# Tail copies on VectorE, one eviction per step, joined q and v loads, and weights written in place, in an attention and gated feed-forward kernel

## The chip, the cores and the metric

The kernel runs on one core of one Trainium2 chip. The metric is the device time of one execution in microseconds (us). The kernel before took 737.65 us, the median of 3 runs (736.29 to 739.47).

## The reference, cut to what matters

```python
# q, k, v: (4 batches, 8 heads, 576 positions, 64), float32
scores = q @ k.T / 8 + bias        # bias per head: a two-layer net of log positions (hidden 32)
attn = exp(scores - max) / (sum + 1e-9)
x = (attn @ v) -> (2304 tokens, 512)
h = x @ w_in                       # (2304, 2048), weights arrive in float64
g = (a0 + a1*h + a2*h^2 + a3*h^3) / (1 + |b0|*|h| + |b1|*h^2 + 1e-6)
out = g @ w_out                    # (2304, 512)
```

## The kernel before, in words

The work has three stages. From 0 to about 54 us a table of the position bias is computed and stored in device memory. From about 54 to 323 us attention runs. After that the feed-forward part runs to the end, at 735.5 us; it multiplies each weight as a high and a low part, since the products run in a reduced 32-bit format.

Attention goes by 16 units of one head pair and one batch (`units`), and a unit has five steps (`steps`, c = 0 to 4). In steps c = 0 to 3 TensorE multiplies 128 query rows of each of the two heads with all 576 keys; in step c = 4 it takes the last 64 rows of both heads at once. The order is written out by hand in `step_a(i)`, and each engine works strictly in that order:

- `e_qk(i)` (L328): the score products, into one PSUM tile `sc` per head, of two banks each. There are only two such buffers, so a step's products for a head must wait until the previous step's tile for that head is no longer read.
- `e_ttr(i, j)` (L356): VectorE adds the bias to `sc`, writes the sum `s2` and its extreme value. `e_exp` (L371): ScalarE takes the exponential.
- `e_tp(i - 2)` (L415): TensorE transposes the exponentials of two steps ago, 64 rows at a time (r = 0, 1). Two of these transposes (the "tails", the last 64 keys) go into free columns of the present step's `sc` tiles (`spare`, L346), the others into `tp`, one bank for each r. ScalarE copies tail r = 0 to `ptl` and both `tp` tiles to `ptm` (L552); VectorE copies tail r = 1 (L564), after both `e_ttr` and, in step c = 0, after the two small operations of `e_recip`. Accesses of two engines to one PSUM bank are put in series: `e_ttr` of head 0 therefore waits for ScalarE's copy of tail r = 0 out of the same tile.
- `e_pv` (L462): products with v, some in each step (`PV_KEYS`). `e_pvout` copies the result, and one unit later `e_norm` multiplies it by the reciprocal sums, which make a trip through device memory (`rs`, `rb`).

SyncE issues nearly all transfers from one queue in written order. Each takes one of eight semaphores in turn and its issue waits until the transfer eight places earlier has landed. Per unit there are the loads of q, k and the 64-row ends `qdg` (`load_qk`, four transfers) and of v and its ends `vdg` (`load_v`, three). Beside attention run the weight jobs (`w_conv`): 128 columns of `w_in` or rows of `w_out` (`f`, `part`) are loaded, split by VectorE and ScalarE into high `wh` and low `wl`, and stored to a scratch tensor `ws` in device memory (`w_out_to`, L105). `w_load` (L217) brings them back into the resident tiles `wih`, `wil`, `woh`, `wol` of a weight group (two `f` each). The loads stand in the SyncE queue at places given by `after` (L641). VectorE's parts of the jobs are spread over the steps by `JOB_OPS`.

Of the kernel before, what the change touches and what calls it, by code (L numbers as in the profile page):

```python
# [8 lines left out]
F32 = mybir.dt.float32  # L9
F32R = mybir.dt.float32r  # L10
# [6 lines left out]
P = 128  # L17
# [17 lines left out]
def tile_attn_moe(  # L35
# [75 lines left out]
    def w_conv(f, part):  # L111
        st = {}

# [48 lines left out]
        def low():  # L162
            V.scalar_tensor_tensor(
                out=tl("wl", F32R), in0=st["wm"], scalar=2.0 ** -36, in1=st["wk"].bitcast(F32),
                op0=ALU.mult, op1=ALU.mult,
            )

        def store():
            w_out_to(
                f, part, st["wh"].rearrange("p (k f) -> p k f", k=KD),  # L170
                st["wl"].rearrange("p (k f) -> p k f", k=KD),
            )
# [48 lines left out]
    with tc.manual_schedule():  # L221
# [3 lines left out]
        with ExitStack() as actx:  # L225
# [3 lines left out]
            ps_tp = actx.enter_context(tc.tile_pool(name="ps_tp", bufs=2, space=PSUM))  # L229
            ps_pv = actx.enter_context(tc.tile_pool(name="ps_pv", bufs=1, space=PSUM))  # L230

            vdg = [cpool.tile([P, P], F32, tag=f"vdg{i}", name=f"vdg{i}") for i in range(3)]
            qdg = [apool.tile([P, P], F32, tag=f"qdg{i}", name=f"qdg{i}") for i in range(2)]
            sums = [apool.tile([P, P], F32, tag=f"sum{i}", name=f"sum{i}") for i in range(2)]
            for t in vdg + qdg + sums:
                G.memset(t, 0.0)
# [21 lines left out]
            def load_qk(u, eng=nc.sync):  # L258
                p, b = units[u]
                q = qkp.tile([P, 512], F32, tag="q", name=f"q{u}")  # L260
                k = qkp.tile([P, KW], F32, tag="k", name=f"k{u}")
                eng.dma_start(out=q, in_=qt[b, p, :, 0:512])
                eng.dma_start(out=k, in_=kt[b, p])
                for j in range(2):
                    r = slice(64 * j, 64 * j + 64)
                    eng.dma_start(out=qdg[u % 2][r, r], in_=qt[b, p, r, 512:S])
                qk[u] = (q, qdg[u % 2], k)

            def load_v(u):
                p, b = units[u]  # L270
                t = qkp.tile([P, 4, P], F32, tag="v", name=f"v{u}", bufs=3)
                nc.sync.dma_start(out=t, in_=vp[b, p, 0:512].rearrange("(c k) d -> k c d", k=P))
                dg = vdg[u % 3]
                for j in range(2):
                    nc.sync.dma_start(
                        out=dg[64 - 64 * j:P - 64 * j, 64 * j:64 * j + 64],
                        in_=vp[b, p, 512:576, 64 * j:64 * j + 64],
                    )
                vt[u] = (t, dg)
# [76 lines left out]
            def e_ttr(i, j):  # L356
                u, c = steps[i]
                p, b = units[u]
                t = epool.tile([P, S], F32, tag="s2", name=f"s2_{i}_{j}")
                m = epool.tile([P, 1], F32, tag="m", name=f"m{i}_{j}", bufs=4)  # L360
                idx = 8 if j == 2 else 4 * j + c
                V.tensor_tensor_reduce(  # L362
                    out=t.rearrange("p (a s) -> p a s", a=2),
                    in0=sc.pop((i, j))[:, :, :SH],
                    in1=bias[p][:, idx, :].rearrange("p (a s) -> p a s", a=2),
                    scale=-0.125, scalar=3.0e38,
                    op0=ALU.add, op1=ALU.min, accum_out=m,
                )
                s2[i, j] = (t, m)
# [45 lines left out]
            def e_tp(i, tl):  # L415
# [7 lines left out]
                ps = [ps_tp.tile([P, 8, 64], F32, tag="tp", name=f"tp{i}_{r}") for r in range(2)]  # L423
# [5 lines left out]
                if c < 4:  # L429
                    for r in range(2):  # L430
                        tr(r, tl[r], 512)
                    for kc in range(4):
                        for j in range(2):
                            for r in range(2):
                                tr(r, ps[r][:, 2 * kc + j, :], (S + 64 if j == 0 else 0) + kc * P)
                    return (
                        [(pl[:, o:o + 64], tl[0])]
                        + [(pm[:, :, :, o + 64 * r:o + 64 * r + 64],
                            ps[r].rearrange("p (k j) s -> p k j s", j=2)) for r in range(2)],
                        [(V.tensor_copy, pl[:, o + 64:o + P], tl[1])], None,  # L440
                    )
# [8 lines left out]
                for r in range(2):  # L450
                    x = slice(64 * r, 64 * r + 64)
                    T.transpose(ps[r][:, 5, :], sm[x, :], ident[x, x])  # L452
                return (
                    [(pm[:, :, r, o:o + 64], ps[r][:, 0:4, :]) for r in range(2)],
                    [(eng, rt[:, 64 * r:64 * r + 64], ps[r][0:9, 5, :])
                     for r, eng in ((0, A.copy), (1, V.tensor_copy))]
                    + [(eng, pl[x, o:o + 64], ps[r][x, 4, :])
                       for r, x, eng in ((0, slice(64, P), A.copy), (1, slice(0, 64), V.tensor_copy))],
# [61 lines left out]
            def step_a(i):  # L520
# [70 lines left out]
            with ExitStack() as bctx:  # L591
# [21 lines left out]
                pc = ps_tp.tile([P, 512], F32, tag="tp", name="pc")  # L613
# [41 lines left out]
                for y, n in enumerate(order):  # L655
# [4 lines left out]
                    if 24 <= n < 32:  # L660
                        ps = ps_tp.tile([P, 512], F32, tag="tp", name=f"pb{n}")
# [40 lines left out]
            w_alloc(wpool, 2)  # L702

# [196 lines left out]
def _layout(inputs):  # L900
# [8 lines left out]
    qt = np.concatenate([q0, q1], axis=2)  # L909
# [7 lines left out]
    vp = np.asarray(inputs["v"]).reshape(B, NP, 2, S, D).transpose(0, 1, 3, 2, 4).reshape(B, NP, S, 2 * D)  # L917
# [49 lines left out]
```

## Time and profile before

| | before |
|---|---|
| median of 3 runs | 737.65 us |
| the profiled execution | 737.32 us, span 735.5 us |
| TensorE matmul busy | 706.6 us (96%) |
| VectorE busy | 594.6 us (81%) |
| ScalarE busy | 515.6 us (70%) |
| GpSimd busy | 187.2 us (25%) |
| share of the chain that ended last | PE 75%, DMA 8%, DVE 5%, ACT 3%, SyncE's queue 2% |

In the profile PE is TensorE, PEld its weight loads, DVE VectorE, ACT ScalarE, POOL GpSimd, SPq the queue of SyncE. Busy time of PE counts a matmul from start to modelled end, so a PE that is "busy" may still be held up inside a row. "[0.41 <-ACT ptl L552]" behind a row says that the engine sat idle for 0.41 us before it and what ended the idle time.

### The profile page before, as it was taken

What the parts mean: (1) busy time and instruction counts of PE and PEld (TensorE: products, weight loads), DVE (VectorE), ACT (ScalarE), POOL (GpSimd) and SP (SyncE); (2) the same over time, 40 slices, a digit from 0 to 9 for tenths busy, and PEclk for the clock granted to TensorE, in tenths of its full rate; (3) what the DMA queues carried; (4) which work ended last, traced back from release to release, by engine and by line L of the source; (5) the groups of instructions that cost most, each with busy time, mean ns of one, the idle gap of its engine ahead of it and who ended that gap; (6) DMA issues with size and microseconds to landing.
All of it is one profiled execution on the core that took longest, in us unless ns stands there. A gap on an engine that the chain in (4) does not pass through costs nothing.

```text
span 735.5 us, 13700 instructions
## 1 busy us (share of the span) xinstructions
PE 706.6 (96%) x4930; PEld 545.4 (74%) x4930; DVE 594.6 (81%) x1068; ACT 515.6 (70%) x969; POOL 187.2 (25%) x127
## 2 busy tenths in 40 slices
PE   6988999998999999899999999999999999999997
PEld 3225666665666566568788999889999899988996
DVE  7995677776677777649999999999997878788766
ACT  6889888887788787757566665767665665556552
POOL 0000000000000000004544444554543444344442
PEclk9999999999899999999999999999999999999999
DMA  4787879988798888847434444457942213031021
GB/s 162 274 317 262 265 250 285 298 270 258 249 310 274 251 291 266 267 118 241 129 129 150 146 145 172 160 173 238 284 166 86 89 40 130 2 128 59 29 86 43
DMA packets 107427, 137.76 MB, mean 187 GB/s; under 512 B 17104, under 2 KB 66528, under 8 KB 107360
## 3 DMA queue, kind: packets, MB, share of 16 engines
q1 hardware_dynamic: 106768, 136.11, 56.6%
q8 instruction: 39, 0.64, 0.4%
q10 hardware_dynamic: 592, 0.78, 0.3%
q14 instruction: 28, 0.23, 0.1%
HBM read 94.96 MB, written 41.90 MB: 186 GB/s over the span
## 4 chain that ended last, share of the span: by engine, by line
PE 75%; DMA 8%; DVE 5%; ACT 3%; issue 2%; SPq 2%; POOL 0%; DVEq 0%; ACTq 0%; POOLq 0%
PE o L803 25%; PE h L316 24%; PE sc L341 10%; PE pv L471 6%; PE tp L427 4%; PE pb L668 3%; DMA k<-in_kt_dram 2%; DVE s L362 1%; PE pv L477 1%; ACT p L382 1%; DMA ws<-wl 1%; DMA wy<-in_w_in_dram 1%; PE sc L427 1%; ACT ptm L552 1%; DMA rs<-rt 1%
## 5 line engine op out<-in xcount | busy, mean ns | idle before, releaser
L362 DVE CUSTOM_DVE_ANT_0 s<-sc,bias 128x576 f32<-128x576 f32 x144 | 104.1, 755 | 71.1 <-ACT ptl L552 61.2
L733 POOL TENSOR_TENSOR u<-u,w 128x768 f32<-128x768 f32 x48 | 96.6, 2013 | 159.3 <-ACT u L731 133.6
L341 PE MATMUL sc<-k,q 64*128 64x288 f32 x512 | 108.4, 439 | 9.9 <-DMA k<-in_kt_dram 4.4
L382 ACT ACTIVATE p<-s,m 128x576 f32<-128x576 f32 x144 | 111.7, 781 | 2.2 <-DVE m L362 1.8
L730 ACT ACTIVATE w<-h 128x768 f32<-128x768 f32 x48 | 39.0, 813 | 100.5 <-PE h L316 98.1
L772 POOL TENSOR_TENSOR gl<-m,r 128x768 fp32r<-128x768 f32 x47 | 87.1, 1853 | 71.5 <-DVE m L765 71.5
L316 PE MATMUL h<-xh,wg 128*128 128x384 f32 x384 | 101.7, 336 | 0.0
L341 PEld LDWEIGHTS sc<-k,q 64*128 64x128 f32 x512 | 60.0, 189 | 55.9 <-issue 23.8
L552 ACT COPY ptm<-tp 128x512 f32<-128x512 f32 (+1 forms) x160 | 79.1, 546 | 23.9 <-PE tp L452 12.6
L471 PE MATMUL pv<-ptm,v 128*64 128x320 f32 (+1 forms) x512 | 80.4, 425 | 0.0
L378 POOL MEMSET p<- 128x64 f32 x16 | 2.4, 151 | 305.7 <-ACT ptl L552 160.4
L803 PE MATMUL o<-wg,gh 128*128 128x512 f32 x288 | 79.0, 391 | 0.0
L737 ACT ACTIVATE r<-u,qc 128x768 f32<-128x768 f32 x48 | 45.1, 940 | 37.9 <-POOL u L733 37.3
L427 PE MATMUL tp<-ident,p 64*128 64x64 f32 x1184 | 70.3, 227 | 1.3 <-DVE ptl L564 0.7
L316 PEld LDWEIGHTS h<-xh,wg 128*128 128x128 f32 x384 | 69.7, 188 | 1.5 <-DMA rb<-rs 0.5
L758 DVE SCALAR_TENSOR_TENSOR m<-u,qc,gh 128x768 f32<-128x768 f32 x48 | 64.6, 1346 | 5.0
L741 DVE TENSOR_TENSOR t<-t,h 128x768 f32<-128x768 f32 x48 | 45.5, 948 | 27.0 <-ACT t L732 16.2
L316 PE MATMUL h<-xh,wih 128*128 128x384 f32 x192 | 64.9, 338 | 0.8 <-DVE t L744 0.8
L427 PEld LDWEIGHTS tp<-ident,p 64*128 64x128 f32 x1184 | 59.7, 140 | 7.9 <-ACT ptm L552 1.2
L316 PE MATMUL h<-xl,wih 128*128 128x384 f32 x192 | 64.7, 337 | 0.3 <-DVE xl L302 0.3
L316 PE MATMUL h<-xh,wil 128*128 128x384 f32 x192 | 64.7, 337 | 0.0
L316 PE MATMUL h<-xl,wg 128*128 128x384 f32 x192 | 64.4, 335 | 0.0
(82 smaller groups left out, 1412.6 us busy)
## 6 DMA issues: line engine op xcount, KB each, us to landing
tab<-e SPq DMA_DIRECT2D x36, 295.5 KB, 3.6
wx<-in_w_in_dram SPq DMA_DIRECT2D x16, 512.0 KB, 5.1
wy<-in_w_in_dram SPq DMA_DIRECT2D x16, 512.0 KB, 5.6
wx<-in_w_out_dram SPq DMA_DIRECT2D x16, 512.0 KB, 4.5
wy<-in_w_out_dram SPq DMA_DIRECT2D x16, 512.0 KB, 4.6
ws<-wh SPq DMA_DIRECT2D x32, 256.0 KB, 2.7
ws<-wl SPq DMA_DIRECT2D x32, 256.0 KB, 3.1
wg<-ws SPq DMA_DIRECT2D x32, 256.0 KB, 5.4
```

Source lines behind the costliest of these rows:

```text
L316: T.matmul(hps[s][:, j, :TT], w[:, k, sl], x[:, k, :], start=(k == 0 and z == 0), stop=(k == KD - 1 and z == 2),)
L341: T.matmul(sc[i, j][:, a, :SH], l, k[r, o + a * SH:o + (a + 1) * SH], start=True, stop=True,)
L362: V.tensor_tensor_reduce(out=t.rearrange("p (a s) -> p a s", a=2), in0=sc.pop((i, j))[:, :, :SH], in1=bias[p][:, idx, :].rearrange("p (a s ...
L382: A.activation(out=prob[i][:, z * S:z * S + S], in_=t, func=AF.Exp, bias=m, scale=-1.0, accum_out=ssum[u][:, k:k + 1],)
L427: T.transpose(out, pb[x, k0:k0 + P], ident[x, x])
L471: T.matmul(ps[64 * j:64 * j + 64, :w], v[:, kc, 64 * j:64 * j + 64], ptm[u, hf][:, kc, j, :w], start=(kc == 0), stop=False,)
L552: A.copy(out=o, in_=x)
L733: G.tensor_tensor(out=u, in0=u, in1=w, op=ALU.mult)
L741: V.tensor_tensor(out=rt[s, "t"], in0=rt[s, "t"], in1=hps[s][:, :, :TT], op=ALU.mult)
L758: V.scalar_tensor_tensor(out=m, in0=rt[s, "u"], scalar=qc, in1=rt[s, "gh"].bitcast(F32), op0=ALU.add, op1=ALU.mult,)
L772: eng.tensor_tensor(out=lo, in0=rt[s, "m"], in1=rt[s, "r0"], op=ALU.mult)
L803: T.matmul(po[n, c], l[:, j, c * P:(c + 1) * P], r[fp][:, j, :], start=(first and x is a), stop=(last and x is z),)
```

## The change

- Tails: both r go to VectorE, in the order `e_ttr` of head 0, tail 0, `e_ttr` of head 1, tail 1 (in step c = 4: `e_ttr`, tail 0, tail 1). `e_recip` now comes behind tail 1. `s2` gets four buffers for three.
- `tp` is one tile of two banks with one buffer; ScalarE evicts it with one copy. For the transposes of c = 4 ScalarE does all the small copies (three), where VectorE did two of four.
- q comes with its 64-row end in one transfer, and v too; the host pads both with zeros.
- For f = 0, 1, 4, 5 (`here`) VectorE writes the low part straight into the resident tile and one transfer copies the high part there from SBUF; the scratch tensor and the later loads of these groups go.
- Two early users of the `tp` buffers take those of `pv`; a small memset of a tile `edge` is added on GpSimd.

On VectorE, a unit's step c = 4 and the next unit's c = 0 (L362 and L361 are the addition with its extreme value, `ptl` a tail copy, `s_15_0` and `s_15_1` the two heads of c = 0). Before:

```order
L362 ISA s_14_2_1371,m_2_1372<-sc_2_1337,bias_322 128x576 [waits DVE_49,Activation_49]
...
L564 COPY ptl_1_1344<-sc_2_1337 128x64
L152 SCALAR_TENSOR_TENSOR wh_0_1341<-wx_0_1016,wh_0_1341 128x512 [waits DMAHW2_49]
L158 TENSOR_SCALAR wk_0_1330<-wh_0_1341 128x512 [waits DVE_49]
L362 ISA s_15_0_1423,m_0_1424<-sc_0_1390,bias_322 128x576 [waits Activation_49]
...
L362 ISA s_15_1_1426,m_1_1427<-sc_1_1391,bias_322 128x576 [waits PE_49]
...
L389 TENSOR_SCALAR sum_112<-sum_112 128x9
L390 RECIPROCAL sum_112<-sum_112 128x9 [waits DVE_49]
L564 COPY ptl_1_1344<-sc_1_1391 128x64
```

The same two steps on VectorE now:

```order
L361 ISA s_14_2_1312,m_2_1313<-sc_2_1281,bias_308 128x576 [waits PE_49,Activation_49]
...
L554 COPY ptl_1_1288<-sc_2_1281 128x64
L555 COPY ptl_1_1288<-sc_2_1281 128x64
L153 SCALAR_TENSOR_TENSOR wh_0_1285<-wx_0_983,wh_0_1285 128x512 [waits DMAHW6_49,Activation_49]
L159 TENSOR_SCALAR wk_0_1274<-wh_0_1285 128x512 [waits DVE_49]
L361 ISA s_15_0_1360,m_0_1361<-sc_0_1330,bias_308 128x576 [waits PE_49]
...
L554 COPY ptl_1_1288<-sc_0_1330 128x64
L361 ISA s_15_1_1364,m_1_1365<-sc_1_1331,bias_308 128x576 [waits PE_49]
...
L555 COPY ptl_1_1288<-sc_1_1331 128x64
L388 TENSOR_SCALAR sum_107<-sum_107 128x9 [waits Activation_49]
L389 RECIPROCAL sum_107<-sum_107 128x9 [waits DVE_49]
```

The first addition of a step waits for TensorE alone where it waited for ScalarE; a tail copy has come in between the two additions, and the last tail copy has moved ahead of the two small operations.

On SyncE, the first loads of a weight group back from the scratch (f = 0, L219). Before:

```order
L107 DMA ws_1_2008<-wh_1_1866 128x512 [waits DMAHW0_49]
L108 DMA ws_1_2008<-wl_1_2006 128x512 [waits DMAHW1_49,DVE_49]
L219 DMA wih_714<-ws_0_1068 128x4x128 [waits DMAHW2_49]
L219 DMA wil_715<-ws_0_1068 128x4x128 [waits DMAHW3_49]
L219 DMA woh_716<-ws_1_1282 128x512 [waits DMAHW4_49]
L219 DMA wol_717<-ws_1_1282 128x512 [waits DMAHW5_49]
L272 DMA v_2017<-in_vp_dram 128x4x128 [waits DMAHW6_49]
L275 DMA vdg_107<-in_vp_dram 64x64 [waits DMAHW7_49]
L275 DMA vdg_107<-in_vp_dram 64x64 [waits DMAHW0_49]
```

The same stretch of the SyncE queue now:

```order
L107 DMA ws_1_1907<-wh_1_1774 128x512 [waits DMAHW2_49]
L108 DMA ws_1_1907<-wl_1_1905 128x512 [waits DMAHW3_49,DVE_49]
L277 DMA v_1912<-in_vp_dram 128x5x128 [waits DMAHW4_49]
L409 DMA xd_75<-xs_1659 128x576 [waits DMAHW5_49,DVE_49]
L396 DMA rb_1960<-rs_1885 64x512 [waits DMAHW6_49,DMAHW1_49]
```

The four loads are gone from between the stores and v, and v is one transfer for three.

The diff, cut to its core:

```diff
@@ -160,12 +161,21 @@
             )
 
         def low():
+            out = w_hilo(f, part)[1] if here else tl("wl", F32R)
+            wm, wk = st["wm"], st["wk"].bitcast(F32)
+            if here:
...
             V.scalar_tensor_tensor(
-                out=tl("wl", F32R), in0=st["wm"], scalar=2.0 ** -36, in1=st["wk"].bitcast(F32),
-                op0=ALU.mult, op1=ALU.mult,
+                out=out, in0=wm, scalar=2.0 ** -36, in1=wk, op0=ALU.mult, op1=ALU.mult
...
         def store():
+            if here:
+                nc.sync.dma_start(
+                    out=w_hilo(f, part)[0].bitcast(F32),
+                    in_=st["wh"].bitcast(F32).rearrange("p (k f) -> p k f", k=KD),
+                )
...
-                q = qkp.tile([P, 512], F32, tag="q", name=f"q{u}")
+                q = qkp.tile([P, KW], F32, tag="q", name=f"q{u}")
                 k = qkp.tile([P, KW], F32, tag="k", name=f"k{u}")
-                eng.dma_start(out=q, in_=qt[b, p, :, 0:512])
+                eng.dma_start(out=q, in_=qt[b, p])
                 eng.dma_start(out=k, in_=kt[b, p])
-                for j in range(2):
-                    r = slice(64 * j, 64 * j + 64)
-                    eng.dma_start(out=qdg[u % 2][r, r], in_=qt[b, p, r, 512:S])
-                qk[u] = (q, qdg[u % 2], k)
+                qk[u] = (q, q[:, 512:KW], k)
 
             def load_v(u):
                 p, b = units[u]
-                t = qkp.tile([P, 4, P], F32, tag="v", name=f"v{u}", bufs=3)
-                nc.sync.dma_start(out=t, in_=vp[b, p, 0:512].rearrange("(c k) d -> k c d", k=P))
-                dg = vdg[u % 3]
-                for j in range(2):
-                    nc.sync.dma_start(
-                        out=dg[64 - 64 * j:P - 64 * j, 64 * j:64 * j + 64],
-                        in_=vp[b, p, 512:576, 64 * j:64 * j + 64],
-                    )
-                vt[u] = (t, dg)
+                t = qkp.tile([P, 5, P], F32, tag="v", name=f"v{u}", bufs=3)
+                nc.sync.dma_start(out=t, in_=vp[b, p].rearrange("(c k) d -> k c d", k=P))
+                vt[u] = (t, t[:, 4])
...
-                t = epool.tile([P, S], F32, tag="s2", name=f"s2_{i}_{j}")
+                t = epool.tile([P, S], F32, tag="s2", name=f"s2_{i}_{j}", bufs=4)
...
-                ps = [ps_tp.tile([P, 8, 64], F32, tag="tp", name=f"tp{i}_{r}") for r in range(2)]
+                ps = ps_tp.tile([P, 2, 8, 64], F32, tag="tp", name=f"tp{i}")
...
-                                tr(r, ps[r][:, 2 * kc + j, :], (S + 64 if j == 0 else 0) + kc * P)
+                                tr(r, ps[:, r, 2 * kc + j], (S + 64 if j == 0 else 0) + kc * P)
+                    to = pm.rearrange("p k j s -> p (k j) s")[:, :, o:o + P]
                     return (
-                        [(pl[:, o:o + 64], tl[0])]
-                        + [(pm[:, :, :, o + 64 * r:o + 64 * r + 64],
-                            ps[r].rearrange("p (k j) s -> p k j s", j=2)) for r in range(2)],
-                        [(V.tensor_copy, pl[:, o + 64:o + P], tl[1])], None,
+                        [(to.rearrange("p x (r s) -> p r x s", r=2), ps)],
+                        [(pl[:, o + 64 * r:o + 64 * r + 64], tl[r]) for r in range(2)], [], None,
...
                 for r in range(2):
                     x = slice(64 * r, 64 * r + 64)
-                    T.transpose(ps[r][:, 5, :], sm[x, :], ident[x, x])
+                    T.transpose(ps[:, r, 5], sm[x, :], ident[x, x])
                 return (
-                    [(pm[:, :, r, o:o + 64], ps[r][:, 0:4, :]) for r in range(2)],
-                    [(eng, rt[:, 64 * r:64 * r + 64], ps[r][0:9, 5, :])
-                     for r, eng in ((0, A.copy), (1, V.tensor_copy))]
-                    + [(eng, pl[x, o:o + 64], ps[r][x, 4, :])
-                       for r, x, eng in ((0, slice(64, P), A.copy), (1, slice(0, 64), V.tensor_copy))],
+                    [(pm[:, :, :, o:o + 64].rearrange("p k r s -> p r k s"), ps[:, :, 0:4])], None,
+                    [(rt.rearrange("p (r s) -> p r s", r=2), ps[0:9, :, 5])]
+                    + [(pl[x, o:o + 64], ps[x, r, 4]) for r, x in ((0, slice(64, P)), (1, slice(0, 64)))],
                     lambda: nc.sync.dma_start(out=rsum[u], in_=rt),
                 )
...
-                    mains, tails, fin = e_tp(i - TL, spare(i) if steps[i - TL][1] < 4 else None)
+                    mains, tl, tails, fin = e_tp(i - TL, spare(i) if steps[i - TL][1] < 4 else None)
                     for o, x in mains:
                         A.copy(out=o, in_=x)
                 for _ in range(PV_KEYS[(i - TL) % 5] if i < NS + TL else len(fill)):
                     if fill:
                         e_pv(*fill.pop(0))
+                vec = [lambda j=j: e_ttr(i, j) for j in heads(i)] if ok(0) else []
+                if ok(TL) and tl:
+                    vec[1:1] = [lambda x=x: V.tensor_copy(out=x[0], in_=x[1]) for x in tl[:1]]
+                    vec += [lambda x=x: V.tensor_copy(out=x[0], in_=x[1]) for x in tl[1:]]
+                for x in vec:
+                    x()
                 if ok(0):
-                    for j in heads(i):
-                        e_ttr(i, j)
                     e_exp(i, heads(i)[0])
                 if ok(1) and steps[i - 1][1] == 4:
                     e_recip(steps[i - 1][0])
                 if ok(TL):
-                    for eng, o, x in tails:
-                        eng(out=o, in_=x)
+                    for o, x in tails:
+                        A.copy(out=o, in_=x)
                     if fin:
                         fin()
...
-                for f in range(2):
-                    after[2 * (f + 2) + 1] = [lambda f=f: [w_load(f, z) for z in range(2)]]
-                for f in range(4, 6):
-                    after[2 * f + 5] = [lambda f=f: [w_load(f, z) for z in range(2)]]
+                for f, y in () if wide else ((0, 5), (1, 7), (4, 13), (5, 15)):
+                    after[y] = [lambda f=f: [w_load(f, z) for z in range(2)]]
...
+            G.memset(wpool.tile([P, 8], F32, tag="edge", name="edge"), 0.0)
...
```

## Rows read from the trace of the kernel before

**Rows 1.** Busy time by stage (us, engines' busy us with instructions, granted clock, DMA share, GB/s).
```profile
116.00:132.00 16.00, 15.72 (x162) 10.16 (x161) 12.03 (x37) 13.94 (x37) 0.15 (x1) 1.00 0.97 299
180.00:196.00 16.00, 13.29 (x115) 9.32 (x117) 8.05 (x25) 9.47 (x26) 0.15 (x1) 0.79 0.83 267
400.00:500.00 100.00, 100.00 (x504) 90.53 (x504) 97.45 (x104) 67.02 (x87) 49.55 (x25) 1.00 0.46 153
```
**Rows 2.** Who waited for whom: us in total, times, longest.
```profile
DVE s L362 <- ACT ptl L552: 61.2, 63, 4.4
```
**Rows 3.** Timeline, third and fourth step of a unit: start us, us, engine, line, operation.
```profile
154.77 0.22 PE L427 MATMUL sc<-ident,p 64*128 64x64 f32 x2
...
155.37 0.21 ACT L552 COPY ptl<-sc 128x64 f32<-128x64 f32 x1
...
155.61 0.76 DVE L362 CUSTOM_DVE_ANT_0 s<-sc,bias 128x576 f32<-128x576 f32 x1 [1.19 <-ACT ptl L552]
...
156.97 0.22 DVE L564 COPY ptl<-sc 128x64 f32<-128x64 f32 x1
...
157.11 0.75 DVE L409 TENSOR_TENSOR xs<-xs,rb 128x576 f32<-128x576 f32 x1
...
157.31 0.54 PEld L341 LDWEIGHTS sc<-k,q 64*128 64x128 f32 x5 [0.37 <-issue]
...
158.38 0.22 PE L427 MATMUL sc<-ident,p 64*128 64x64 f32 x1
...
158.86 0.76 DVE L362 CUSTOM_DVE_ANT_0 s<-sc,bias 128x576 f32<-128x576 f32 x1 [0.41 <-ACT ptl L552]
```
**Rows 4.** Timeline, the unit's fifth step and the next unit's first.
```profile
161.96 0.27 PE L427 MATMUL sc<-ident,p 64*128 64x64 f32 x2
...
162.58 0.76 DVE L362 CUSTOM_DVE_ANT_0 s<-sc,bias 128x576 f32<-128x576 f32 x1 [0.68 <-ACT ptl L552]
...
164.67 0.22 PE L427 MATMUL sc<-ident,p 64*128 64x64 f32 x1
...
165.35 0.76 DVE L362 CUSTOM_DVE_ANT_0 s<-sc,bias 128x576 f32<-128x576 f32 x1 [1.21 <-ACT ptl L552]
...
167.05 0.16 DVE L564 COPY ptl<-sc 128x64 f32<-128x64 f32 x1
...
167.33 0.54 PEld L341 LDWEIGHTS sc<-k,q 64*128 64x128 f32 x5 [0.70 <-issue]
```
**Rows 5.** Timeline of VectorE, the one reciprocal of each unit.
```profile
134.76 0.22 DVE L390 RECIPROCAL sum<-sum 128x9 f32<-128x9 f32 x1
...
150.73 0.22 DVE L390 RECIPROCAL sum<-sum 128x9 f32<-128x9 f32 x1
...
166.92 0.22 DVE L390 RECIPROCAL sum<-sum 128x9 f32<-128x9 f32 x1
...
186.64 0.21 DVE L390 RECIPROCAL sum<-sum 128x9 f32<-128x9 f32 x1
...
204.34 0.21 DVE L390 RECIPROCAL sum<-sum 128x9 f32<-128x9 f32 x1
...
236.29 0.22 DVE L390 RECIPROCAL sum<-sum 128x9 f32<-128x9 f32 x1
...
253.55 0.22 DVE L390 RECIPROCAL sum<-sum 128x9 f32<-128x9 f32 x1
...
269.53 0.22 DVE L390 RECIPROCAL sum<-sum 128x9 f32<-128x9 f32 x1
...
320.34 0.21 DVE L390 RECIPROCAL sum<-sum 128x9 f32<-128x9 f32 x1
```
**Rows 6.** The chain that ended last, where the first loads back stand (start us, us, what).
```profile
167.96 8.02 DMA ws<-wl
```
**Rows 7.** Groups by line and shape: count, busy us, mean ns, idle before.
```profile
L552 ACT COPY ptm<-tp 128x512 f32<-128x512 f32 x128 | 68.8, 590 | 10.9 <-PE tp L427 10.6
...
L564 DVE COPY ptl<-sc 128x64 f32<-128x64 f32 x63 | 13.0, 206 | 0.0
```

More of the change, by code (lines that the diff above doesn't have):

```diff
@@ L112, in w_conv @@
         st = {}
+        here = f < KH and f // 2 in (0, 2)
         def load():
@@ L162, in low @@
         def low():
+            out = w_hilo(f, part)[1] if here else tl("wl", F32R)
+            wm, wk = st["wm"], st["wk"].bitcast(F32)
+            if here:
+                wm, wk = (x.rearrange("p (k f) -> p k f", k=KD) for x in (wm, wk))
             V.scalar_tensor_tensor(
-                out=tl("wl", F32R), in0=st["wm"], scalar=2.0 ** -36, in1=st["wk"].bitcast(F32),
-                op0=ALU.mult, op1=ALU.mult,
+                out=out, in0=wm, scalar=2.0 ** -36, in1=wk, op0=ALU.mult, op1=ALU.mult
             )
         def store():
+            if here:
[3 more added lines that the diff above has]
+                )
+                return
             w_out_to(
@@ L228, in tile_attn_moe @@
             epool = actx.enter_context(tc.tile_pool(name="epool", bufs=3))
-            ps_tp = actx.enter_context(tc.tile_pool(name="ps_tp", bufs=2, space=PSUM))
+            ps_tp = actx.enter_context(tc.tile_pool(name="ps_tp", bufs=1, space=PSUM))
             ps_pv = actx.enter_context(tc.tile_pool(name="ps_pv", bufs=1, space=PSUM))
-            vdg = [cpool.tile([P, P], F32, tag=f"vdg{i}", name=f"vdg{i}") for i in range(3)]
-            qdg = [apool.tile([P, P], F32, tag=f"qdg{i}", name=f"qdg{i}") for i in range(2)]
             sums = [apool.tile([P, P], F32, tag=f"sum{i}", name=f"sum{i}") for i in range(2)]
-            for t in vdg + qdg + sums:
+            for t in sums:
                 G.memset(t, 0.0)
@@ L443, in e_tp @@
                     for r in range(2):
-                        tr(r, ps[r][:, kc, :], kc * P)
+                        tr(r, ps[:, r, kc], kc * P)
                 for r in range(2):
-                    tr(r, ps[r][:, 4, :], 448 + 64 * r)
+                    tr(r, ps[:, r, 4], 448 + 64 * r)
                 sm = ssum.pop(u)
@@ L612, in tile_attn_moe @@
                 A.activation(out=bts, in_=pts, func=AF.Identity, scale=b1s)
-                pc = ps_tp.tile([P, 512], F32, tag="tp", name="pc")
+                pc = ps_pv.tile([P, 512], F32, tag="pv1", name="pc")
                 T.matmul(pc[:, 0:1], w28, b1s, start=True, stop=True)
@@ L660, in tile_attn_moe @@
                     if 24 <= n < 32:
-                        ps = ps_tp.tile([P, 512], F32, tag="tp", name=f"pb{n}")
+                        ps = ps_pv.tile([P, 512], F32, tag=f"pv{n % 2}", name=f"pb{n}")
                     else:
@@ L908, in _layout @@
     k0, k1 = pairs(inputs["k"])
-    qt = np.concatenate([q0, q1], axis=2)
+    pad = np.zeros((B, NP, D, 64), np.float32)
+    qt = np.concatenate(
+        [
+            np.concatenate([q0, pad], axis=-1),
+            np.concatenate([q1[..., :512], pad, q1[..., 512:]], axis=-1),
+        ],
+        axis=2,
+    )
     kt = np.concatenate(
@@ L916, in _layout @@
     )
-    vp = np.asarray(inputs["v"]).reshape(B, NP, 2, S, D).transpose(0, 1, 3, 2, 4).reshape(B, NP, S, 2 * D)
+    v = np.asarray(inputs["v"]).reshape(B, NP, 2, S, D)
+    v0, v1 = v[:, :, 0], v[:, :, 1]
+    pad = np.zeros((B, NP, 64, D), np.float32)
+    vp = np.concatenate(
+        [
+            np.concatenate([v0[:, :, :512], pad, v0[:, :, 512:]], axis=2),
+            np.concatenate([v1, pad], axis=2),
+        ],
+        axis=3,
+    )
     g = np.arange(4)
```

## The prediction

> **What bounds the kernel now.** I read the busy times by stage first. From 400 us on TensorE is busy all the time at the full clock [rows 1]; the change touches no line of that stage, so whatever it brings must come out of attention. There TensorE is nearly as busy (15.72 of 16 us from 116 to 132 us), but a busy row may hold a stall, so the list of waits came next: VectorE's additions waited 61.2 us in 63 places for ScalarE's tail copy [rows 2], nearly 1 us a step. Whether that costs the end anything, the timeline tells. In a unit's third step the two tail transposes end at 154.77 + 0.22 = 154.99 us; ScalarE, behind its exponentials, copies tail 0 only at 155.37, and the first addition starts at 155.61. Tail 1 is copied at 156.97, 1.36 us later, and only after it TensorE's weights for the second head load (157.31, after 0.37 us idle); the next tails end at 158.60 and the next addition starts at 158.86 [rows 3]. So two-head steps form a ring: additions, tail 1, second head's products, tails, ScalarE's copy, additions. Last I read the reciprocals, one per unit, as a ruler: a unit takes 15.97 us (134.76 to 150.73), but 19.72 and 17.70 us from 166.92 and from 186.64, and 17.26 us from 236.29 [rows 5].
>
> **The change, part by part.**
>
> *Tails on VectorE.* The first addition may start when TensorE's tails have ended. The gaps from there to its start are 155.61 - 154.99 = 0.62 us in the third step, 158.86 - 158.60 = 0.26 in the fourth [rows 3], 162.58 - 162.23 = 0.35 in the fifth and 165.35 - 164.89 = 0.46 in the next unit's first [rows 4]. Of each some 0.03 us stays as a hop. Against it stands tail 0 between the additions. A tail copy lasts 0.22 us, but the next VectorE operation starts 0.14 us after its start (156.97 to 157.11) [rows 3]; I take 0.14. The Trainium skill, page "VectorE: DVE Perf Modes", section "The DRAIN you can't avoid", says that the next operation starts only when the pipe has emptied. By that a tail would cost its whole 0.22 us, the three places below 0.24 us less a unit, and the time would be 3.6 us longer; the row speaks against it, for a tail with another kind of operation behind it.
>
> In the first step the two small operations of `e_recip` also move behind tail 1: before, tail 1 starts 167.05 - 165.35 = 1.70 us after the first addition [rows 4], against 1.36 in the third step [rows 3], so 0.34 us go.
>
> What of this reaches TensorE? From third to fourth step tail 1 ends 0.62 - 0.03 - 0.14 = 0.45 us earlier; the idle time there is 0.37 us, so I count 0.37. From first to second it is 0.46 - 0.03 - 0.14 + 0.34 = 0.63 us, out of an idle time of 0.70 [rows 4]. From fifth to first the one addition, then both tails: 0.35 - 0.03 - 0.14 = 0.18 us. In the fourth step TensorE has more products with v, and I count nothing; nor in the second, where no tails go into `sc`. Sum: 1.18 us a unit, or 15 x 1.18 = 17.7 us. Bounds: nothing, if another wait holds the additions; 0.62 + 0.26 + 0.35 + 0.46 + 0.34 = 2.03 us a unit, if all of it came through. What is queued behind tail 0 on VectorE is the second addition, and behind that ScalarE's exponential, which is read two steps later; its 0.14 us are hidden there. VectorE's jobs between tail 1 and the next addition leave 0.41 us idle in the fourth step [rows 3], so they just fit.
>
> *One eviction from the two-bank tile.* Two copies take 68.8 / 128 = 0.54 us each in busy time, 1.07 us together; one copy lies between 0.59 us (the mean of one row) and these 1.07 [rows 7], and I take 1.0. It is on ScalarE, which is busy 13.94 of 16 us [rows 1] and loses four tail copies a unit too. The next transposes into that tile come about 2 us after it ends, so I cost it at nothing, either way. Without that cover TensorE would wait at most 0.5 us a step for the second bank. The small copies for the fifth step that go from VectorE to ScalarE are two of 0.2 us a unit, behind an exponential, and hidden likewise. The memset and the borrowed `pv` buffers lie where GpSimd and these buffers are idle: nothing, at worst 0.2 us once.
>
> *Weights in place.* The first loads back stand behind a store that took 8.02 us on the chain [rows 6]: SyncE's queue has eight transfers under way, and the k of the next unit waits behind them. The three long units cost 3.75 + 1.73 + 1.29 = 6.8 us over 15.97 [rows 5], the middle one because the clock fell to 0.79 after the stall [rows 1]. All three follow loads of f = 0 and 1, which go. The three units from 269.53 to 320.34 take 50.81 us, 2.9 over [rows 5]; loads of f = 4 and 5 stand there and go, those of f = 2 and 3 stay. I count half, 1.4. Sum 8.2 us; bounds 3.75 (the worst stall alone) and 9.7 (all).
>
> *q and v in one transfer* take four issues a unit out of the queue. They lie beside TensorE's work in a unit of 15.97 us; I count them in the 8.2.
>
> *What comes late next.* With 8 jobs the change saves three transfers of 256 KB each out of four (two stores and two loads become one copy), 6.3 MB; at 299 GB/s that is 21 us of transfer time, about what attention is to shorten. So the transfers stay as dense as they are, up to 0.97 of the time [rows 1], and the jobs of f = 2, 3 and 6 to 9 still take the scratch. I take 4 us for units in which k or a weight lands late; bounds 0 and 10 (below). The trace has no copy from SBUF to SBUF, whose pieces are 512 bytes for half of them; by the store of the same bytes it costs what a store costs. The Trainium skill, page "DMA: Bandwidth & Descriptors", section "Why small descriptors are slow (HBM only)", says that such copies do not suffer from small pieces. By that I would take 2 us less; no row shows it.
>
> Sum: 17.7 + 8.2 - 4 = 21.9 us. The profiled execution took 737.3 us, so 715.4; the median of the runs stands 0.3 above that execution: 716 us.
>
> **The rivals.**
>
> 1. *The transfers become the bound.* For it: a share of 0.97 in a dense unit, which is 15.5 us of 16. If no unit gets under 15.5 us, the ring brings 0.5 x 15 = 7.5 us and the loads 8.2: 722 us. Against it: the bytes fall with the time.
> 2. *The additions stay late.* ScalarE's exponentials set when `s2` buffers come free, and VectorE's jobs have 0.41 us of room [rows 3]; if either holds the first addition where it is, only the loads pay: 737.7 - 8.2 = 729 us. Against it: the fourth `s2` buffer, and that 61.2 us are put down to the copy alone [rows 2].
> 3. *Slower: the ring grows by the tails.* Tail 0 and a later tail 1 stand in the ring of four steps a unit. If the start of the additions does not come forward and each tail costs 0.22 us, that is 4 x 0.22 x 15 = 13.2 us, against 8.2 from the loads: 743 us. It decides where a tail costs more than the start gains, on the mean (0.62 + 0.26 + 0.35 + 0.46) / 4 = 0.42 us; the rows show 0.14 to 0.22, and in the fourth step the gain is only 0.26.
> 4. *More.* All 2.03 us a unit and all 9.7 us of long units, with no price: 15 x 2.03 + 9.7 = 40 us at most; TensorE's own work would stop it on the way. I put it at 704 us.
>
> **How the numbers follow.** Forecast 0.62, with a range of its own of 709 to 721; rival 1 0.16; rival 2 0.12; rival 3 0.05; rival 4 0.05. The range of 8 in 10 reaches to rivals 1 and 2 and towards the fourth: 706 to 729 us. A difference under 0.5% (3.7 us) can hardly be told from none for this kernel. Faster: 0.61 + 0.16 + 0.05 and 0.08 of rival 2, 0.90; within 0.5%: 0.05; slower: 0.05.
>
> **What would show it.** Right: VectorE's wait for ScalarE's tail copy is gone and its idle time before additions falls well under 61 us, ended by TensorE; the reciprocals stand 14.8 to 15 us apart; no unit after the loads of f = 0 is long and the clock does not fall; the stage from the first gated step on takes as long as before. Wrong: reciprocals still 15.9 us apart (rival 2), 15.5 us apart with k or the weight loads as releasers (rival 1), or over 16 us with TensorE waiting for tail copies (rival 3). A feed-forward stage of another length would make the whole account wrong.

## The result, and the profile after

The changed kernel took 712.41 us, the median of 4 runs (711.34 to 713.59), against 736.97 us for four runs of the kernel before: ratio 0.9669, 95% interval 0.9627 to 0.9710. Of the profiled executions the span went from 735.5 to 711.5 us, 24.0 us less.

Where the 24.0 us come from is read with the ruler of the prediction, the reciprocals of VectorE, one per unit. Before, they ran from 69.83 to 320.34 us, after from 72.56 to 296.90. So the first unit ends 2.7 us later, the 15 units between take 224.3 us instead of 250.5 (26.2 less), and from the last reciprocal to the end it is 414.6 us instead of 415.2.

The long units of [rows 5], 166.92 to 186.64 and 186.64 to 204.34, have as their counterparts 162.96 to 178.05 and 178.05 to 193.14 (VectorE's timeline of the changed kernel, with the unit ahead of them):

```profile
147.87 0.22 DVE L389 RECIPROCAL sum<-sum 128x9 f32<-128x9 f32 x1
...
162.96 0.22 DVE L389 RECIPROCAL sum<-sum 128x9 f32<-128x9 f32 x1
...
178.05 0.22 DVE L389 RECIPROCAL sum<-sum 128x9 f32<-128x9 f32 x1
...
193.14 0.22 DVE L389 RECIPROCAL sum<-sum 128x9 f32<-128x9 f32 x1
```

They stand 15.09 us apart. On the chain that ended last, where [rows 6] had a store of 8.02 us, the transfers' share is 1% now (8% before):

```profile
PE 84%; DVE 3%; issue 1%; DMA 1%; ACT 0%; SPq 0%; POOL 0%; DVEq 0%; ACTq 0%; POOLq 0%
```

The windows of the changed kernel answer to [rows 1]: us, the engines' busy us with instructions, granted clock, DMA share, GB/s.

```profile
116.00:132.00 16.00, 16.00 (x179) 11.09 (x177) 13.35 (x42) 13.47 (x29) 0.15 (x1) 1.00 0.85 283
180.00:196.00 16.00, 16.00 (x170) 10.86 (x166) 13.24 (x42) 14.10 (x31) 0.15 (x1) 1.00 0.82 252
400.00:500.00 100.00, 100.00 (x504) 90.74 (x503) 97.46 (x104) 66.57 (x87) 48.96 (x24) 1.00 0.58 185
```

In the second window TensorE was busy for 13.29 us at a clock of 0.79 before; now it is busy throughout at 1.00. The share of the transfers fell from 0.97 to 0.85 in the first.

The list of waits of the changed kernel, VectorE's additions (us in total, times, longest), answers to [rows 2]:

```profile
DVE s L361 <- PE sc L426: 31.0, 54, 1.5
...
DVE s L361 <- ACT wh L145: 5.1, 6, 1.0
...
DVE s L361 <- PE sc L340: 4.5, 10, 0.9
...
DVE s L361 <- DMA bias<-tab: 2.9, 1, 2.9
```

The 61.2 us for ScalarE's tail copy are gone. Most of what is left ends with TensorE's own tail transposes (L426), which is where the ring should end.

The timeline of the changed kernel, third to fifth step of a unit, answers to [rows 3]:

```profile
151.50 0.22 PE L426 MATMUL sc<-ident,p 64*128 64x64 f32 x2
...
151.77 0.76 DVE L361 CUSTOM_DVE_ANT_0 s<-sc,bias 128x576 f32<-128x576 f32 x1 [0.81 <-PE sc L426]
...
152.45 0.22 DVE L554 COPY ptl<-sc 128x64 f32<-128x64 f32 x1
...
152.59 0.75 DVE L361 CUSTOM_DVE_ANT_0 s<-sc,bias 128x576 f32<-128x576 f32 x1
...
153.26 0.22 DVE L555 COPY ptl<-sc 128x64 f32<-128x64 f32 x1
...
153.47 0.91 PEld L340 LDWEIGHTS sc<-k,q 64*128 64x128 f32 x8 [0.49 <-issue]
...
154.67 0.22 PE L426 MATMUL sc<-ident,p 64*128 64x64 f32 x1
...
154.91 0.76 DVE L361 CUSTOM_DVE_ANT_0 s<-sc,bias 128x576 f32<-128x576 f32 x1 [0.16 <-PE sc L426]
...
158.25 0.28 PE L426 MATMUL sc<-ident,p 64*128 64x64 f32 x2
...
158.68 0.76 DVE L361 CUSTOM_DVE_ANT_0 s<-sc,bias 128x576 f32<-128x576 f32 x1 [0.60 <-PE sc L426]
```

The first addition starts 151.77 - 151.72 = 0.05 us behind the end of the tails, 0.02 us in the fourth step and 0.15 in the fifth, where it was 0.62, 0.26 and 0.35. Tail 0 holds VectorE for 152.59 - 152.45 = 0.14 us and lies between the additions.

### The profile page after: what moved, and what is told of

Read it like the earlier page. It is cut to its first block, busy times and chain, and to the rows that moved or that the text cites. A ratio compares the mean times of both kernels' runs of the same rounds, so it can differ in the third digit from the quotient of the medians.

```text
span 711.5 us, 13532 instructions
## 1 busy us (share of the span) xinstructions
PE 691.0 (97%) x4930; PEld 546.1 (77%) x4930; DVE 597.8 (84%) x1100; ACT 500.7 (70%) x841; POOL 192.8 (27%) x123
## 4 chain that ended last, share of the span: by engine, by line
PE 84%; DVE 3%; issue 1%; DMA 1%; ACT 0%; SPq 0%; POOL 0%; DVEq 0%; ACTq 0%; POOLq 0%
PE o L802 26%; PE h L315 25%; PE sc L340 13%; PE pv L467 10%; PE tp L426 6%; PE pv L473 2%; PE sc L426 1%; DVE gh L750 1%; DMA xr<-xd 1%; DVE m L757 1%; DVE t L743 0%; DVE t L740 0%; DVE wm L148 0%; DVE wk L159 0%; POOL gl L771 0%
## 5 line engine op out<-in xcount | busy, mean ns | idle before, releaser
L361 DVE CUSTOM_DVE_ANT_0 s<-sc,bias 128x576 f32<-128x576 f32 x144 | 107.3, 754 | 46.2 <-PE sc L426 31.0
L340 PE MATMUL sc<-k,q 64*128 64x288 f32 (+1 forms) x576 | 114.9, 429 | 3.1 <-DVE ptl L554 2.6
L340 PEld LDWEIGHTS sc<-k,q 64*128 64x128 f32 (+1 forms) x576 | 69.4, 187 | 45.2 <-issue 24.4
L548 ACT COPY ptm<-tp 128x1024 f32<-128x1024 f32 (+1 forms) x80 | 74.0, 926 | 37.7 <-PE tp L426 28.7
L750 DVE SCALAR_TENSOR_TENSOR gh<-t,cst,r 128x768 fp32r<-128x768 f32 x48 | 58.2, 1212 | 9.3 <-ACT r L737 6.9
L426 PE MATMUL tp<-ident,p 64*128 64x64 f32 x1184 | 64.4, 226 | 0.4 <-ACT ptm L548 0.4
```

The lines of the kernel that those rows point to most:

```text
L340: T.matmul(sc[i, j][:, a, :SH], l, k[r, o + a * SH:o + (a + 1) * SH], start=True, stop=True,)
L361: V.tensor_tensor_reduce(out=t.rearrange("p (a s) -> p a s", a=2), in0=sc.pop((i, j))[:, :, :SH], in1=bias[p][:, idx, :].rearrange("p (a s ...
L426: T.transpose(out, pb[x, k0:k0 + P], ident[x, x])
L750: V.scalar_tensor_tensor(out=hi, in0=rt[s, "t"], scalar=abs_[:, 0:1], in1=rt[s, "r0"], op0=ALU.add, op1=ALU.mult,)
```

## The experiments

The ruler for all of them: spacing of the reciprocals in us, the profiled execution of each kernel. Each ratio is against runs of the kernel before that were made beside it; their medians were 736.25 to 738.81 us, so differences of about a microsecond between two experiments say nothing.

| kernel | first at | most units | longer units | last at |
|---|---|---|---|---|
| before | 69.83 | 15.97 to 16.79 | 19.72, 17.70, 17.26, 17.07, the last 16.95 | 320.34 |
| after | 72.56 | 14.97 to 15.18, the last 13.27 | none | 296.90 |
| tails alone | 70.59 | 14.98 to 15.10 | 18.68, 20.45, 16.56, 16.86, 20.66, 16.16, 16.89, 17.19 | 319.54 |
| transfers alone | 70.45 | 15.97 to 16.81, the last 14.53 | none | 311.80 |
| q, v undone | 70.64 | 14.98 to 15.10, the last 13.50 | 18.86 | 298.92 |
| in place undone | 70.93 | 14.98 to 15.10 | 15.91, 19.11, 15.35, 15.85, 18.77, 15.28, 16.90, 17.50 | 311.11 |
| tail 0 on ScalarE | 70.98 | 15.71 to 16.48, the last 14.31 | none | 307.99 |

**Tails alone**: the changed kernel with both edits of transfers undone.

```diff
-        here = f < KH and f // 2 in (0, 2)
+        here = False
-    eng.dma_start(out=q, in_=qt[b, p])
+    eng.dma_start(out=q, in_=qt[b, p, :, 0:512])
+    for j in range(2): ... eng.dma_start(out=qdg[u % 2][r, r], ...)
```

> The changed kernel with both transfer edits undone: q and v in parts as before, all weights through the scratch and loaded back. Theory (ring and queue are two separate gains): units 15.1 us apart where nothing is late, as in the changed kernel, so 15 x 0.89 = 13 us less than before, about 724 us; the long units after the first loads back stay. Rival (the transfers alone gave the gain, the tails ride on them): units 15.9 us apart, about 735 us.

Measured 738.74 us, ratio 1.0002 (0.9978 to 1.0026): no gain at all. The quiet units have the changed kernel's length, so the ring is shorter; but eight units are long, together 22.8 us over 15.08 each, and that gives it back: 15 units in 248.95 us, where before took 250.5. The list of waits of this kernel (L351 is the score product) names what they wait for, the timeline shows two of these waits, and the windows show what stands beside them.

```profile
PE sc L351 <- DMA k<-in_kt_dram: 12.8, 4, 4.4
```

```profile
153.65 0.65 SPq L273 DMA_DIRECT2D k<-in_kt_dram  x1
...
161.37 1.33 PE L351 MATMUL sc<-k,q 64*128 64x288 f32 x8 [3.12 <-DMA k<-in_kt_dram]
...
180.78 1.90 PE L351 MATMUL sc<-k,q 64*128 64x288 f32 x6 [4.44 <-DMA k<-in_kt_dram]
```

```profile
130.00:160.00 30.00, 28.25 (x292) 18.53 (x288) 23.84 (x74) 25.29 (x55) 0.31 (x2) 1.00 0.94 297
160.00:190.00 30.00, 24.19 (x231) 17.02 (x233) 17.26 (x53) 17.33 (x40) 0.15 (x1) 0.89 0.86 255
163.00:176.00 13.00, 13.00 (x142) 8.63 (x136) 10.90 (x33) 11.05 (x25) 0.15 (x1) 1.00 0.88 260
182.00:184.00 2.00, 2.00 (x24) 1.77 (x20) 0.78 (x3) 0.00 (x0) 0.00 (x0) 0.50 0.95 298
```

k is issued at 153.65 and is there 7.7 us later; TensorE was ready 3.12 us before. Behind this stall the granted clock stays at 1.00; behind the next one, of 4.44 us, it is 0.50. So the 0.89 from 160 to 190 us is a mean of time at 1.00 (2.4 GHz) and time at 0.50 (1.2 GHz), as the 0.79 of [rows 1] is, and the slow time stretches the unit too. k is late here because it is issued late: from issue to landing it takes 7.7 us on the median, and 7.1 in the changed kernel, but there, from the second unit on, it is issued between 2.6 us ahead of a unit's reciprocal and 1.5 us behind it, here 7.7 us behind it (153.65) and 9.4 (174.03). What in SyncE's queue holds the issue back, the places or the landing of earlier transfers, was not tried apart.

The theory that counted the ring's gain by itself is refuted. The expectation's rival is nearer in time (about 735 us), but its units of 15.9 us do not occur where nothing is late. It is the prediction's first rival in kind, with the transfers taking the gain back, though not by its figure: units under 15.5 us do occur.

**Transfers alone**: the changed kernel's loads and weights in place; tails, the two evictions and three `s2` buffers as before.

```diff
-  vec[1:1] = [... V.tensor_copy ... tl[:1]]
-  vec += [... V.tensor_copy ... tl[1:]]
+  [(pl[:, o:o + 64], tl[0])] + ... # ScalarE, ahead of the two evictions
+  [(V.tensor_copy, pl[:, o + 64:o + P], tl[1])]
```

> The changed kernel with the tails, the two-bank tile and the fourth s2 buffer undone; only the transfer edits stay. Theory: units 15.97 us apart but no long ones: the 10 to 12.8 us of long units go, less 2 us that the first unit lost, 726 to 729 us. Rival (transfers alone gave the gain): 715 us, units near 15.1.

728.83 us, ratio 0.9883 (0.9860 to 0.9905). All long units are gone, the quiet ones are unchanged: 15 units in 241.35 us, 9.2 less than before. The tails on top bring 241.35 - 224.34 = 17.0 us.

**q and v undone**, weights in place kept (the second half of the first diff).

> The changed kernel with q and v in parts as before. Theory: nothing waits for these four transfers in the attention stage, so the units stay 15.08 us apart; the 2.9 us wait for the bias in the first unit goes if it came from weight loads issued sooner behind the shorter q and v, then 710 us, else 712. Rival (the freed places in the queue removed the long units): some units over 16 us, 715 to 718 us.

718.01 us, ratio 0.9742 (0.9703 to 0.9782): 5.6 us slower than the change. One unit of fifteen, the 14th, is long. In it VectorE waits for the reciprocal sums back from device memory, ahead of its additions, and TensorE then idles 1.67 us:

```profile
269.03 0.76 DVE L419 TENSOR_TENSOR xs<-xs,rb 128x576 f32<-128x576 f32 x1 [2.25 <-DMA rb<-rs]
```

So the places in SyncE's queue matter, but rarely.

**Weights in place undone**, q and v joined.

```diff
-        here = f < KH and f // 2 in (0, 2)
+        here = False
-    for f, y in () if wide else ((0, 5), (1, 7), (4, 13), (5, 15)):
+    for f, y in ((0, 5), (1, 7), (4, 13), (5, 15)):
```

> The changed kernel with the four f through the scratch and loaded back as before. Theory: the long units after the loads back return, 7 to 12 us, 720 to 724 us, one of them with the clock below 1.00; quiet units stay at 15.08. Rival (the joined q and v keep the queue clear): no long unit, 712 to 714 us.

727.41 us, ratio 0.9886 (0.9844 to 0.9927): 15 us slower. TensorE waits for k again:

```profile
PE sc L340 <- DMA k<-in_kt_dram: 7.7, 4, 3.1
```

Of the transfers' edits this is the one that carries the gain.

**Tail 0 back on ScalarE**, all else as changed.

```diff
-    for o, x in mains:
+    for o, x in (tl[:1] if tl else []) + mains:
         A.copy(out=o, in_=x)
-    vec[1:1] = [... tl[:1]]
```

> The changed kernel with tail 0 copied by ScalarE ahead of the eviction, as before; all else stays, also tail 1 ahead of the reciprocal. Theory (ScalarE's lateness is what the ring lost): VectorE's additions wait for ScalarE's copy again, 0.7 us a unit more than 15.08 after the 0.14 us of tail 0 are taken off, units near 15.7, 720 to 724 us. Rival (the order of reciprocal and tail 1 and the fourth s2 buffer gave the gain): units 15.1 to 15.3, 712 to 715 us.

723.68 us, ratio 0.9828 (0.9811 to 0.9846). The wait of [rows 2] is back in this kernel:

```profile
DVE s L361 <- ACT ptl L548: 58.2, 62, 2.0
```

Its units repeat every five (15.86, 15.71, 16.48, 15.72, 15.71), as before's do (16.19, 15.98, 16.80, 15.98, 15.98 in the run of transfers alone): I read it as ScalarE's part of the weight jobs, which stands ahead of the tail copy in two units of five; this was not tried by itself. With tail 0 on VectorE the pattern is gone. So ScalarE's lateness is shown to be the cost: the 15 units take 237.0 us for 224.3, and tail 0 carries 12.7 of the 17.0 us.

**Two evictions** from two one-bank tiles, all else as changed but for the two early users, which go back to the `tp` buffers.

```diff
-    ps = ps_tp.tile([P, 2, 8, 64], F32, tag="tp", name=f"tp{i}")
+    ps = [ps_tp.tile([P, 8, 64], F32, tag="tp", name=f"tp{i}_{r}") for r in range(2)]
```

> The changed kernel with two one-bank tiles for the transposes and two copies out of them, as before; tails on VectorE stay. Theory (the merged eviction is off the path): units 15.08 us apart, 712 to 713 us, ScalarE busier by 0.07 us a step. Rival (the merged copy gives a part of the gain): units 15.2 to 15.4, 714 to 717 us.

714.03 us (712.08 to 715.13), units 15.09 as in the change and a profiled span of 710.3 us: the joined eviction is off the path. The median lies in the rival's range, but its ratio, 0.9696 (0.9674 to 0.9719), is not told apart from the change's.

**Reciprocals ahead of tail 1**, as the kernel before had them.

```diff
+    if ok(1) and steps[i - 1][1] == 4:
+        vec.append(lambda: e_recip(steps[i - 1][0]))
     vec += [... tl[1:]]
```

> The changed kernel with the two small operations on the sums ahead of tail 1, as before. Theory: the ring from a unit's first to its second step grows by 0.34 us, units 15.4 us apart, 716 to 718 us. Rival (TensorE has other work there): 15.08, 712 us.

718.23 us, ratio 0.9753 (0.9730 to 0.9776), units 15.36: 0.28 us a unit, 4.2 in fifteen. With tail 0's 12.7 that is 16.9 of the 17.0 us that the tails bring.

**Weight jobs two steps later** (`if i >= 4:` for `if i >= 2:` ahead of `run_jobs`), because the first unit of the change waits 2.9 us for its bias.

> The changed kernel with the first weight loads issued two steps later. Theory (the weight loads behind the shorter q and v delay the bias of the first unit): the wait of 2.9 us for the bias goes, the first reciprocal stands at 70.5 us, 710 us. Rival (one late landing in one execution): 712 us, whether the wait is seen or not.

711.94 us, ratio 0.9672 (0.9656 to 0.9688). The wait for the bias stayed, 2.6 us, so the first weight loads don't cause it. It is there in every version but two (two evictions, and the fifth step's copies on VectorE below), with tails alone (2.2 us) and with transfers alone (2.4), so it needs neither half of the change; why it is there, I can't say. The first reciprocal does come earlier here, at 71.09 us for 72.56, and the rows show why. The changed kernel, behind the wait for the bias:

```profile
64.41 0.76 DVE L361 CUSTOM_DVE_ANT_0 s<-sc,bias 128x576 f32<-128x576 f32 x1 [2.92 <-DMA bias<-tab]
...
65.46 2.26 PE L340 MATMUL sc<-k,q 128*128 128x288 f32 x4 [2.06 <-DVE ptl L554]
```

```profile
65.40:67.80 2.40, 2.34 (x6) 1.33 (x8) 0.72 (x3) 1.49 (x4) 0.00 (x0) 0.50 1.07 351
```

The same four products in this run:

```profile
65.25 1.21 PE L340 MATMUL sc<-k,q 128*128 128x288 f32 x4 [1.74 <-DVE ptl L554]
```

TensorE idles 2.06 us behind the bias in the change, the granted clock is 0.50 behind that, and the products take 2.26 us; here it idles 1.74 us and they take 1.21. That is 1.05 of the 1.47 us.

**The fifth step's tail copies on VectorE too.**

```diff
-    for o, x in tails:
-        A.copy(out=o, in_=x)
+    for n_, (o, x) in enumerate(tails):
+        (A.copy if n_ < 1 else V.tensor_copy)(out=o, in_=x)
```

> The changed kernel with the two copies of tails that the fifth step left on ScalarE moved to VectorE too. Theory (ScalarE's copies are no longer the last release of the addition behind the fifth step): units 15.0 to 15.1, the whole 711 to 712.5. Rival (ScalarE still ends last there, once in a unit): units 14.8 to 14.9, the whole 708 to 710.

719.33 us, ratio 0.9738 (0.9704 to 0.9773), units 15.38 to 15.74: a miss of both. The timeline of this kernel shows a new wait:

```profile
166.85 0.24 ACT L564 COPY rt<-tp 9x128 f32<-9x128 f32 x1
...
167.12 0.46 DVE L564 COPY ptl<-tp 64x64 f32<-64x64 f32 x2 [0.85 <-ACT rt L564]
...
168.17 0.74 DVE L361 CUSTOM_DVE_ANT_0 s<-sc,bias 128x576 f32<-128x576 f32 x1
```

```profile
DVE ptl L564 <- ACT rt L564: 16.9, 16, 4.2
```

VectorE's pair of copies waits for ScalarE's first copy out of the same tile of banks, which comes behind exponentials; 16 such waits make 16.9 us (the list of waits, second fence), and the next addition queues behind them. A copy moved to the other engine brought back the coupling that the change removes.

**Three `s2` buffers** instead of four.

> The changed kernel with three buffers for the sums of scores and bias instead of four. Theory (the fourth is not used, since ScalarE's exponentials free a buffer in time): no change, units 15.08, 712 plus or minus 1. Rival (it is part of the gain): additions wait for exponentials, units 15.2 to 15.9, 715 to 725.

712.9 us, units 14.98 to 15.09, the last two 15.17 and 13.28: the fourth buffer is not needed.

**Tail 0 in another bank**: from the eleventh step on its transposes go to free columns of the bank of the last `pv`, and VectorE takes both additions first.

```diff
-    return [sc[...]...]
+    t = pvt["last", hf]
+    return [t[:, o:o + 64], y[:, SH:SH + 64]]
-    vec[1:1] = [... tl[:1]]
-    vec += [... tl[1:]]
+    vec += [... tl[::-1]]
```

> The changed kernel, with tail 0's transposes written, from the eleventh step on, to free columns of the bank of the last output step's accumulation instead of to the second half of a score bank, and with tail 0 behind the additions on VectorE, so that a step's first addition stands behind no tail. In the changed kernel the additions still wait 31 us in 54 waits for TensorE's scores. Theory (VectorE's row of tail 0, additions, tail 1 and reciprocal is what is left in the ring): the units go from 15.08 us to 14.3 to 14.6, the whole to about 702 to 706. Rival (the remaining wait is for TensorE's own work, which is the same): the units stay within 0.1 of 15.08, the whole at 711 to 713.

712.3 us (707.71 to 717.27), ratio 0.9648 (0.9579 to 0.9717). Thirteen units take 14.52 to 14.87 us, 0.4 less than in the change, which speaks for the theory; but the last two take 15.44 and 15.97, and the whole is the change's. The timeline shows what gave it back: ScalarE's first split of the feed-forward input waits for its load (issued at 276.21), with the unit's exponentials queued behind it.

```profile
276.21 0.57 SPq L289 DMA_DIRECT2D xr<-xd  x1
...
282.00 0.51 ACT L300 CAST xh<-xr 128x384 fp32r<-128x384 f32 x1 [2.76 <-DMA xr<-xd]
282.42 0.77 ACT L388 ACTIVATE p<-s,m 128x576 f32<-128x576 f32 x1
```

**The same with that load one step earlier** (`i == NS - 9` for `NS - 8` ahead of `load_x(0, 0)`).

> The kernel of the experiment with tail 0's transposes in the output's bank, and the first load of the feed-forward stage's input issued one attention step earlier, ahead of the last v. In that experiment the units went to 14.66 us but the last two took 15.44 and 15.97, with a wait of 2.8 us of ScalarE for that load, in front of its exponentials, and one of 1.45 for scores before it. Theory (the load is what is late there, and the faster units then reach the end): no wait over 1 us of ScalarE for the load, the last two units together 28.0 to 29.5 us instead of 31.4, the whole 707 to 710.5. Rival (an earlier load makes k or v late in its place, since the DMA queue is what is full): last units as long as before, a wait for k or v instead, the whole 711 to 714.

The last units take 14.74 and 13.14 us, 27.9 together, the last reciprocal comes at 290.93, 6.0 us before the change's, and the profiled span is 707.4 us. From there to the end it is 416.5 us, 1.9 more than after the change. The timed runs don't settle a gain: 711.6 us median (709.18 to 715.15, clocks 0.992 to 0.998), ratio 0.9664 (0.9631 to 0.9698), against 0.9669 (0.9627 to 0.9710). No version is shown to beat the change.

## Why the prediction came out right

It said 716 us, with 709 to 721 as its own range; 712.41 was measured. Step by step:

- *Ring, 1.18 us a unit, 17.7 in all.* Measured on top of the transfers: 17.0 us, or 1.13 a unit. Undoing the two steps one by one gives 12.7 (tail 0) and 4.2 (reciprocals). The places can be read on TensorE, from the end of one step's tails to the end of the next one's, in the unit of [rows 3] and [rows 4] and its counterpart. The third to fifth steps stand there and in the fence above; the first steps around them are these, before:

```profile
148.69 0.22 PE L427 MATMUL sc<-ident,p 64*128 64x64 f32 x1
```

After:

```profile
145.82 0.22 PE L426 MATMUL sc<-ident,p 64*128 64x64 f32 x1
...
160.90 0.22 PE L426 MATMUL sc<-ident,p 64*128 64x64 f32 x1
...
161.13 0.76 DVE L361 CUSTOM_DVE_ANT_0 s<-sc,bias 128x576 f32<-128x576 f32 x1 [0.75 <-PE sc L426]
```

| from, to | before | after | less | predicted |
|---|---|---|---|---|
| first, third step | 154.99 - 148.91 = 6.08 | 151.72 - 146.04 = 5.68 | 0.40 | 0.63 |
| third, fourth | 158.60 - 154.99 = 3.61 | 154.89 - 151.72 = 3.17 | 0.44 | 0.37 |
| fourth, fifth | 162.23 - 158.60 = 3.63 | 158.53 - 154.89 = 3.64 | -0.01 | 0 |
| fifth, first | 164.89 - 162.23 = 2.66 | 161.12 - 158.53 = 2.59 | 0.07 | 0.18 |

The additions came forward as predicted, in the first step too (0.01 us behind the tails, for 0.46). But in this unit the sum is 0.90, not 1.18: the step with the reciprocals was priced too high and so was the fifth. The rest of the 1.13 is the pattern of five, which the prediction didn't see: with the transfers alone a unit takes 15.97 to 16.81 us, and in the change all but the last two take 14.97 to 15.09, whatever their place in the pattern. So the mechanism is right, and that 17.7 fits 17.0 so closely is luck in part. The units stand 15.08 us apart, just outside the 14.8 to 15 that the prediction gave as its sign.
- *Tail 0 costs 0.14 us.* It does: 152.45 to 152.59. The Trainium skill, page "VectorE: DVE Perf Modes", section "The DRAIN you can't avoid", would by its first rule have the addition wait for the copy's whole 0.22 us; it adds that an operation that isn't held starts earlier, and that is what the trace of the change shows, with an addition behind the tail too.
- *Reciprocals behind tail 1, 0.34 us a unit.* 0.28, by undoing it.
- *Loads, 8.2 us.* 9.2 with the transfers alone, the long units gone altogether. Its parts were misread. These are the issues of the second and the third loads back, of f = 1 and f = 4, in the kernel before:

```profile
168.38 0.54 SPq L219 DMA_DIRECT2D wih<-ws  x1
...
239.00 0.89 SPq L219 DMA_DIRECT2D wih<-ws  x1
```

The store of 8.02 us stands ahead of the loads of f = 1; those of f = 0 (141.54) lie in a unit of 15.97 us and cost nothing. The third long unit follows f = 4, not f = 0 or 1, and in the last three units only f = 5 (269.38) goes; f = 2 and 3 (287.75 and 305.59) stay. Against the same units with the transfers alone the first three long ones cost 3.75 + 0.89 + 1.07 = 5.7 us, not 6.8, since the pattern of five was counted in, and the last three 3.5, where 1.4 was counted. The two misses nearly cancel.
- *Eviction and `s2`, nothing.* Nothing that the runs can tell, by undoing each.
- *Price of 4 us for transfers.* No unit of the change is long, so nothing of it was paid there; but the first unit lost 2.7 us, which no step had. 0.5 of it lies ahead of the first addition (54.67 for 54.15); the rest goes with the late bias (2.9 us in one wait) and the clock of 0.50 behind it. The account in spans: 26.2 - 2.7 + 0.6 (from the last reciprocal on), or 24.0 us before rounding, where 21.9 was predicted.

What the sum hides is that its two gains are not independent. Tails alone bring 0.3 us of span (735.5 to 735.2), transfers alone 8.5 (to 727.0), both 24.0. The terms were right only in the order in which they were put, with the loads gone first; "the transfers stay as dense as they are" stood in the text and was the reason, but it was priced as a loss of 4 us and not as a condition of the 17.7. Rival 1 is, in kind, what the faster ring ran into where the weights were not written in place (tails alone, and weights in place undone). Rival 2 would have been right for transfers alone (728.83 against 729). Rival 3 failed at its condition: the additions did come forward, by more than the tails cost.

## What to carry to other kernels

When engines and transfers are both near their bound, a faster ring pays only as far as its next input lands in time: undo each part alone before adding gains, and price the coupling as a condition. In an in-order queue an instruction's own length matters less than what the engine has in front of it: a 0.22 us copy in each of four steps cost 0.85 us a unit on ScalarE behind exponentials, and two more copies on VectorE cost 0.47 us a unit when they had to wait for one of ScalarE's. And after each gain look at the place where the stage ends; a load placed by step count is late when the steps become shorter.

## What was not expected of the hardware

- One copy of 128x1024 from two banks on ScalarE takes 1011 ns on the mean, two of 128x512 took 590 each [rows 7]; the rows of the change:

```profile
L548 ACT COPY ptm<-tp 128x1024 f32<-128x1024 f32 x64 | 64.7, 1011 | 30.4 <-PE tp L426 28.7
...
L554 DVE COPY ptl<-sc 128x64 f32<-128x64 f32 x63 | 13.8, 220 | 0.0
L555 DVE COPY ptl<-sc 128x64 f32<-128x64 f32 x63 | 13.7, 218 | 0.0
```

- In the stretches read, the clock fell only behind stalls, but not behind each: with the tails alone it was 1.00 behind an idle time of 3.12 us and 0.50 behind one of 4.44; in the change 0.50 behind 2.06 us in the first unit, and 1.00 from 160 to 190 us, where nothing stalled. So a late load can be paid twice, once as a wait and once in the clock behind it. No run here shows what decides it.
- The joined copy from SBUF to SBUF was never waited for in the change. What it costs on the transfer engines was not measured by itself.
- The memset on GpSimd, priced at 0.2 us at worst, has a record of 5.94 us, at 48.09. No instruction of the trace waits for it, and no run leaves it out, so whether the 0.5 us ahead of the first addition have to do with it stays open.
